# Four query-feature tasks moved from a gate pass to the down product, with later exponentials, copied-out gates and late stores

## The chip, the cores and the metric

The kernel runs on one core of one Trainium2 chip. The metric is the device time of one execution in microseconds (us). The engines are TensorE (PE), VectorE (DVE), ScalarE (ACT), GpSimd (POOL) and SyncE (SP), whose queue issues nearly all transfers. Each works through its own instructions in order and waits for others by semaphores.

## The reference

A token matrix x of 2048 rows and 1024 columns is layer-normed; the result xn goes through a linear attention with learned features, and through a gated unit; both results are combined with x.

```python
qkv = xn @ wqkv                          # 32 heads of 32
pq, pk = q @ w_phi, k @ w_phi            # per head
phi_q = concat([softmax(pq), softmax(-pq)])
phi_k = concat([softmax(pk), softmax(-pk)])
kv = phi_k^T v ;  z = sum over rows of phi_k
o = (phi_q kv) / (phi_q z + 1e-6)
s = o @ wo
g = silu((sigmoid(xn @ w_gate) * (xn @ w_up)) @ w_down)   # 3584 columns inside
out = x + s * g
```

Everything is fp32. A softmax pair over the 32 values of a head is computed as: the maximum and the minimum (the extremes), the two differences (the spread), the exponential of both, sums and their inverses.

## The kernel before

**Products.** A matrix product in fp32 is made of three matmuls (`mm3`, lines 145 to 147). Each operand is first split (`split`, lines 136 and 137): ACT casts it to the short form, DVE subtracts that from the original. A large product is cut into 2 x 2 blocks and done with seven block products in place of eight; they are named B11, B21, T1 to T4 and B22, and partial results are carried from one to the next in the eight PSUM banks.

**Stages, in order of time.** Layer norm and the weights' sums (to about 310 us, with the first projections among them), the first gate pass (about 310 to 580), projections (to 820), the second gate pass (T2, T3 and T4 of the gated unit, to 1300), the third (T1 and B22, to 1593), the down product (112 steps of `dsteps`, 2352 matmuls, to 2134), and last the attention's output with the product by `wo`, eight pairs of row tiles, whose order is written out word by word in the lists `PAIR` and `LAST`.

**Order of the work.** Around the matmuls stands a plan: `later(n, f)` puts a piece of work n ticks ahead, and `tick()` is called between groups of matmuls and runs what is due. In the down product a tick is 12 matmuls, 2.72 us; in the nests of the third pass 18 ticks are 65 us. A scheduler then sets the final order on each engine; a piece of work may be held to a place behind matmuls already written.

**Feature tasks.** Raw keys, queries and values lie in `qkv_d`. A key task (`k_steps`, second pass) loads a tile, takes extremes, spread, exponential (line 677), inverses, scales, and ends in the key products `kv_products` on PE, which read the low halves that line 729 writes. A query task handles row tile t and column half hb, 32 tasks in all. `q_steps` (early) makes extremes (lines 663 and 664), spread (673 and 674), exponential and inverses (682 and 683) during a gate pass and stores the exponentials in `e_d` and the inverses in `r_d`. `q_late` runs in the down product for all 32 tasks: a light one only loads `e_d` and `r_d`; a heavy one loads the raw queries and does the features there. Both then weigh with z (POOL, line 995), form the density (DVE, 1000 to 1006), scale (POOL, 1013) and store to `e_d`. In the kernel before, the tasks of t = 0 to 7 are early: t up to 5 in the first pass, t = 6 and 7 in the third.

**Nests of the third pass.** A gate product is itself done by seven smaller block products. In `nest`, line 1612 (`nc.scalar.copy(a, c)` in the middle of `product(T3, ...)` and `product(T4, ...)`) copies one bank to another on ACT; the matmuls of T4 wait for it. `h_added` (lines 1437 to 1439) adds on DVE and takes the sigmoid on ACT.

**The second pass.** `keep_bank` (line 1396) copies a bank out on ACT and `seed` (line 1392) copies a stored part into a bank; the next matmuls into that bank wait for either.

**The down product.** Operands are loaded, split by `down_prep` into free buffers some steps ahead, and used in the order of `dsteps`. When a product's last step has written bank p, `evacuate(i, p)` takes the bank's result out. `gate_out` forms silu as y times sigmoid(y) and stores to `g_d`.

**The end.** In `PAIR`, a word eUH loads a tile of `e_d` into buffer U (`e_load`, line 1042), trUHQ transposes it on PE (line 1052), and w0 to w3 load `wo` for B22 into the block `x0` (line 1037) in the first pair. That block held results of the down product before.

Of the kernel before, what the change touches and what calls it, by code (L numbers as in the profile page):

```python
# [11 lines left out]
F32R = mybir.dt.float32r  # L12
AF = mybir.ActivationFunctionType
# [14 lines left out]
HB = 512  # L28
# [21 lines left out]
def hedgehog_glu_kernel(  # L50
# [63 lines left out]
    LEAD = 2  # L114
    KAT, CQ = 0, 7
    BEHIND = 'DVE', 'Activation', 'SP'
# [314 lines left out]
    FLY = range(2, NJ - 1)  # L431
    WD_B, WD_C = range(10), ()
    last_raw, raw_free, spare, groups, made_sums = [], deque(), [], deque(), {}
# [242 lines left out]
    def exponentials(e):  # L676
        nc.scalar.activation(e, e, AF.Exp)  # L677
# [61 lines left out]
    def k_steps(at, hb, t):  # L739

        wide = int((hb, t) >= (0, EARLY))
        for n, f in ((0, k_load), (4, k_extremes), (5, k_spread), (7, lambda *a: exponentials(e_k)),
                     (9, k_inverses), (10, k_scale), (11, k_low), (13 + (1 + wide) * (t < TT - 1), kv_products)):
            later(max(at + n, 1), f, hb, t)
# [202 lines left out]
    def q_steps(at, t, hb):  # L947

        def load():
            p, e = hold[:] = qf_raw.next(), whole(qf_e.next())  # L950
            nc.sync.dma_start(p, qkv_d[Q, t, hb])

        def first():
            hold.append(extremes(f"q{t}{hb}", hold[0]))

        def sums():
            hold.append(inverses(hold[2], hold[1]))

        def keep():
            nc.sync.dma_start(r_d[t, hb], hold[3])  # L960
            nc.sync.dma_start(e_d[t, hb], hold[1])

        hold = []
        for n, f in ((0, load), (5, first), (6, lambda: spread(hold[2], *hold[:2])), (7, lambda: exponentials(hold[1])),
                     (8, sums), (9, keep)):
            later(at + n, f)

    def q_late(at, t, hb):
# [3 lines left out]
        def load():  # L972
            if t < CTT:
                hold["e"] = whole(eqr.next())
                nc.sync.dma_start(hold["e"], e_d[t, hb])
                hold["r"] = small.tile([P, 32], F32, name=f"r{t}{hb}", tag="r", bufs=2)
                nc.sync.dma_start(hold["r"], r_d[t, hb])
            else:
                hold["p"] = qraw.next()
                nc.sync.dma_start(hold["p"], qkv_d[Q, t, hb])  # L980
# [37 lines left out]
        heavy = ((5, first), (6, second), (9, lambda: exponentials(hold["e"])), (11, sums))  # L1018
        steps = ((0, load),) + heavy if t >= CTT else ((6, load),)
        for n, f in steps + ((11, weigh), (14, density), (15, scale), (18, keep)):  # L1020
# [440 lines left out]
    def begin_pass(p):  # L1461

        if p == 0:
# [6 lines left out]
            for n in range(12):  # L1470
                q_steps(5 + 6 * n, n // 2, n % 2)
            for n, f, *a in ((1, x_nest_sums, 0, 1), (2, x_nest_split, 0, T2, (1,)), (2, x_nest_split, 0, T3, (1,)),
# [3 lines left out]
        elif p == 1:  # L1476
            gates_r.items = halves(45, 46)
            gates_r.n = 0
            for n, f, *a in ((152, x_nest_load, 2, 0, 0), (153, x_nest_load, 2, 0, 1), (154, x_nest_load, 2, 1, 0),
                             (159, x_nest_load, 2, 1, 1), (158, x_nest_sums, 2, 0), (163, x_nest_sums, 2, 1),  # L1480
                             (164, x_nest_split, 2, T4, (0,)), (165, x_nest_split, 2, T4, (1,)), (166, x_nest_split, 2, T2), (169, x_nest_split, 2, T3)):
                later(n, f, *a)
            at = KAT
            for t in range(EARLY, 2 * TT):
                k_steps(at, *divmod(t, TT))
                at += 6
                if t % TT == TT - 1:
                    k_end(at + 7, t // TT)
                    at += 18
        else:  # L1490
            for n, j in enumerate(WD_C):
                queue2(40 + 16 * n, wd_sums, j, halves(53, 54))
            qf_raw.items, qf_e.items = [slots[50][:, 1]], [52]
            for n in range(4):
                q_steps(CQ + 18 * n, 6 + n // 2, n % 2)

# [293 lines left out]

    def gate_out(y, t, i, fused=None):

        if fused is None:
            m = sig_r.next()
            nc.scalar.activation(m, y, AF.Sigmoid)
            nc.gpsimd.tensor_mul(y, y, m)  # L1796
        else:
            nc.scalar.activation(y, fused, AF.Sigmoid)
            nc.vector.tensor_mul(y, y, fused)
        nc.sync.dma_start(g_d[t, :, i * HB:(i + 1) * HB], y)  # L1800

    def evacuate(i, p):
# [10 lines left out]
        elif i in (T2, T3):  # L1813
            nc.scalar.copy((u1 if i == T2 else u2)[p], b)
        elif i == T4:
            gate_out(yr.next(), t + 4, 0, b)
        elif i == T1:
            nc.vector.tensor_add(u2[p], u2[p], b)
            later(1 + p, gate_out, u2[p], t + 4, 1)
        else:  # L1820
            nc.vector.tensor_add(u1[p], u1[p], b)
            gate_out(u1[p], t, 1)
# [3 lines left out]
    for hb in range(2):  # L1826
        later(1 + hb, nc.sync.dma_start, zb[hb], zb_d[hb])
    for n in range(TT):
        for hb in range(2):
            q_late(2 + (2 * n + hb) * 24 // 5, n // 2 + n % 2 * CTT, hb)  # L1830
    for n, (i, j, cs) in enumerate(dsteps):
# [52 lines left out]
    res.items = halves(49, 52, 43, 38)  # L1884
    block("x0", 0, 4, F32R)

# [88 lines left out]
    def last_block():  # L1975
# [7 lines left out]
        for h in halved:  # L1983
            nc.vector.tensor_mul(y[:, h], g[:, h], ps[:, h])
            nc.vector.tensor_add(y[:, h], y[:, h], left[:, h])  # L1985
            nc.sync.dma_start(out[t * P:(t + 1) * P, cols.start + h.start:cols.start + h.stop], y[:, h])

    operand_of = dict(B11=B11, B21=B21, T2=T2, T3=T3, T4=T4, T1=T1, B22=B22)
    i_ = lambda n: operand_of[n]
# [11 lines left out]
        (r"y(\w+)", False, lambda p, i: store(p, i_(i))),  # L2001
        (r"w(\d)", False, lambda p, k: p or wo_prep(B22, int(k))),
        (r"rest", False, lambda p: last_rest()),
# [47 lines left out]
```

## Time and profile before

| | us |
|---|---|
| median of three runs | 2351.31 |
| lowest, highest | 2346.94, 2352.96 |
| profiled execution, own time | 2349.81 |
| its span in the trace | 2348.0 |
| mean granted PE clock | 0.998 |

| engine | busy us | share |
|---|---|---|
| PE | 2328.9 | 99% |
| DVE | 1691.8 | 72% |
| ACT | 1246.7 | 53% |
| POOL | 1114.6 | 47% |
| DMA queue q1 | | 78.4% of 16 engines |

A row of the timeline gives the start, the duration, the engine, the line of the kernel, the operation with the tiles written and read, and in brackets the idle time before it and what ended that. A row of a stretch gives busy time and the count of instructions of each engine, then the granted clock of PE, the share of the DMA engines and GB/s. A row of a group gives count, total, mean in nanoseconds, and idle time before.

### The profile page before, as it was taken

How to read it: one execution, taken by the hardware profiler on the slowest of the kernel's cores; microseconds unless marked ns; L12 is line 12 of the kernel's file. 1: busy time of each engine (PE TensorE's matmuls, PEld its weight loads, DVE VectorE, ACT ScalarE, POOL GpSimd, SP SyncE). 2: the span in 40 equal slices, each digit the busy share in tenths (PEclk: the TensorE clock that was granted, in tenths of full speed). 3: DMA queues.
4: the chain of work that ended last, by engine and by line, in shares of the span. 5: the costliest groups of instructions: out<-in, count | busy, mean ns of one | idle time of the engine just before them, and what ended most of it. 6: DMA issues, size and time to landing. Idle time of an engine off the chain costs nothing. (4 is left out here: it accounts for less than half of the span.)

```text
span 2348.0 us, 32662 instructions
## 1 busy us (share of the span) xinstructions
PE 2328.9 (99%) x10816; PEld 1941.1 (83%) x10816; DVE 1691.8 (72%) x2147; ACT 1246.7 (53%) x2003; POOL 1114.6 (47%) x801
## 2 busy tenths in 40 slices
PE   9999999999999999999999999999999999999999
PEld 8888888888888888888888878778888888888887
DVE  8625677776888764777864766674899889876776
ACT  7354577776555555555555555553444444355553
POOL 0323436781231054664663667654665434424556
PEclk9999999999999999999999999999999999999999
DMA  8789987988888777897896877769877667785665
GB/s 298 255 310 360 339 292 275 352 317 300 280 275 286 267 252 271 303 312 256 279 323 204 294 251 237 239 240 354 289 255 262 227 205 253 251 278 199 204 199 184
DMA packets 305017, 635.68 MB, mean 271 GB/s; under 512 B 38608, under 2 KB 38864, under 8 KB 300240
## 3 DMA queue, kind: packets, MB, share of 16 engines
q1 hardware_dynamic: 304848, 633.60, 78.4%
q8 instruction: 84, 1.38, 0.2%
q14 instruction: 85, 0.70, 0.1%
HBM read 380.50 MB, written 252.97 MB: 270 GB/s over the span
## 5 line engine op out<-in xcount | busy, mean ns | idle before, releaser
L145 PE MATMUL bank<-x,w 128*128 128x512 f32 x2248 | 875.9, 390 | 2.4 <-ACT fc L1396 1.9
L146 PE MATMUL bank<-x,w 128*128 128x512 f32 x2248 | 876.0, 390 | 0.0
L147 PE MATMUL bank<-x,w 128*128 128x512 f32 x2248 | 875.1, 390 | 0.0
L137 DVE TENSOR_TENSOR w<-fa,w 128x512 fp32r<-128x512 f32 (+2 forms) x394 | 390.2, 996 | 298.4 <-ACT w L136 288.3
L145 PEld LDWEIGHTS bank<-x,w 128*128 128x128 f32 x2248 | 422.9, 188 | 90.4 <-ACT fc L1396 2.3
L147 PEld LDWEIGHTS bank<-x,w 128*128 128x128 f32 x2248 | 422.6, 188 | 87.4
L146 PEld LDWEIGHTS bank<-x,w 128*128 128x128 f32 x2248 | 422.6, 188 | 87.2
L136 ACT CAST w<-fa 128x512 fp32r<-128x512 f32 (+2 forms) x394 | 268.8, 684 | 335.9 <-PE bank L146 221.3
L145 PE MATMUL bank<-w,x 128*128 128x512 f32 x708 | 277.4, 392 | 0.0
L147 PE MATMUL bank<-w,x 128*128 128x512 f32 x708 | 276.1, 390 | 0.0
L146 PE MATMUL bank<-w,x 128*128 128x512 f32 x708 | 276.0, 390 | 0.0
L137 DVE TENSOR_TENSOR w<-fb,w 128x512 fp32r<-128x512 f32 (+1 forms) x116 | 106.4, 918 | 78.8 <-ACT w L136 78.6
L147 PEld LDWEIGHTS bank<-w,x 128*128 128x128 f32 x708 | 132.9, 188 | 27.7 <-DVE x L1252 0.3
L146 PEld LDWEIGHTS bank<-w,x 128*128 128x128 f32 x708 | 133.0, 188 | 26.8 <-DVE w L1262 0.4
L145 PEld LDWEIGHTS bank<-w,x 128*128 128x128 f32 x708 | 133.1, 188 | 26.1
L136 ACT CAST w<-fb 128x512 fp32r<-128x512 f32 (+1 forms) x116 | 70.2, 605 | 113.7 <-PE bank L146 90.3
L137 DVE TENSOR_TENSOR x<-fb,x 128x512 fp32r<-128x512 f32 (+1 forms) x87 | 88.6, 1022 | 25.0 <-ACT x L136 24.5
L1396 ACT COPY fc<-bank 128x512 f32<-128x512 f32 x116 | 66.5, 584 | 40.6 <-PE bank L147 18.7
L137 DVE TENSOR_TENSOR p<-fc,p 128x512 fp32r<-128x512 f32 (+1 forms) x68 | 50.8, 758 | 40.2 <-ACT p L136 38.2
L1090 POOL TENSOR_TENSOR fc<-fc 128x512 f32<-128x512 f32 x32 | 48.8, 1526 | 62.3 <-DVE fb L1101 20.4
L136 ACT CAST x<-fb 128x512 fp32r<-128x512 f32 (+1 forms) x87 | 65.4, 754 | 12.7 <-DMA fb<-xr_d 5.5
L677 ACT ACTIVATE fc<-fc 128x1024 f32<-128x1024 f32 x36 | 38.2, 1061 | 48.8 <-DVE fc L674 48.6
(412 smaller groups left out, 3822.5 us busy)
## 6 DMA issues: line engine op xcount, KB each, us to landing
m_d<-fc SPq DMA_DIRECT2D x168, 256.0 KB, 4.2
fa<-h_d SPq DMA_DIRECT2D x152, 256.0 KB, 4.3
fa<-wf_d SPq DMA_DIRECT2D x32, 1024.0 KB, 6.8
x<-m_d SPq DMA_DIRECT2D x128, 256.0 KB, 4.9
fa<-w_gu SPq DMA_DIRECT2D x102, 256.0 KB, 5.1
h_d<-fc SPq DMA_DIRECT2D x102, 256.0 KB, 5.0
fc<-e_d SPq DMA_DIRECT2D x48, 512.0 KB, 5.7
fc<-qkv_d SPq DMA_DIRECT2D x88, 256.0 KB, 5.1
```

Source lines behind the costliest of these rows:

```text
L136: nc.scalar.copy(o[0], src)
L137: i = nc.vector.tensor_sub(o[1], src, o[0].bitcast(F32))
L145: nc.tensor.matmul(o, a[0], b[0], start=first, stop=False, **kw)
L146: nc.tensor.matmul(o, a[0], b[1], start=False, stop=False, **kw)
L147: last_mm[:] = [nc.tensor.matmul(o, a[1], b[0], start=False, stop=last, **kw).ins]
L677: nc.scalar.activation(e, e, AF.Exp)
L1090: nc.gpsimd.tensor_sub(o, a, b)
L1396: nc.scalar.copy(o, banks[b])
```

## The change

Line numbers of the changed kernel are a few lower behind line 1480 (1612 becomes 1606, 1800 becomes 1792, 1900 becomes 1897).

1. Query tasks of t = 6 and 7, both halves, are no longer done in the third pass. `QA = 6` takes the place of `CTT` (8) in `q_late`, so that there are 12 light and 20 heavy tasks in the down product, where there were 16 and 16. They no longer alternate: of eight tasks in a row, the third, the sixth and the eighth are light.
2. In key tasks and in early query tasks the exponential comes three ticks after the spread for keys and two for queries, one more than before. The early query tasks as a whole start a tick sooner, so that load, extremes and spread come a tick sooner and the rest at the same tick as before.
3. T4's results in the down product are copied out of their banks, odd ones by ACT and even ones by DVE. Then `gate_out` is put on the plan (sigmoid on ACT, product on POOL). Before, ACT took the sigmoid from the bank and DVE multiplied with the bank.
4. The last four stores to `g_d` that the down product makes for B22 (tiles 8 to 11) wait in a list until w0 in the first pair, ahead of the loads of `wo` into `x0`.

```diff
-    KAT, CQ = 0, 7
+    QA = 6
...
     def k_steps(at, hb, t):
-        for n, f in ((0, k_load), (4, k_extremes), (5, k_spread), (7, lambda *a: exponentials(e_k)),
+        for n, f in ((0, k_load), (4, k_extremes), (5, k_spread), (8, lambda *a: exponentials(e_k)),
                      (9, k_inverses), (10, k_scale), (11, k_low), (13 + (1 + wide) * (t < TT - 1), kv_products)):
...
-        for n, f in ((0, load), (5, first), (6, lambda: spread(hold[2], *hold[:2])), (7, lambda: exponentials(hold[1])),
-                     (8, sums), (9, keep)):
+        for n, f in ((0, load), (5, first), (6, lambda: spread(hold[2], *hold[:2])), (8, lambda: exponentials(hold[1])),
+                     (9, sums), (10, keep)):
             later(at + n, f)
...
     def q_late(at, t, hb):
-            if t < CTT:
+            if t < QA:
...
-        steps = ((0, load),) + heavy if t >= CTT else ((6, load),)
+        steps = ((0, load),) + heavy if t >= QA else ((6, load),)
...
-                q_steps(5 + 6 * n, n // 2, n % 2)
+                q_steps(4 + 6 * n, n // 2, n % 2)
...
-        else:
-            for n, j in enumerate(WD_C):
-                queue2(40 + 16 * n, wd_sums, j, halves(53, 54))
-            qf_raw.items, qf_e.items = [slots[50][:, 1]], [52]
-            for n in range(4):
-                q_steps(CQ + 18 * n, 6 + n // 2, n % 2)
...
+    last_stores = []
+
+    def gate_out(y, t, i):
+
+        m = sig_r.next()
+        nc.scalar.activation(m, y, AF.Sigmoid)
+        nc.gpsimd.tensor_mul(y, y, m)
+        store = lambda: nc.sync.dma_start(g_d[t, :, i * HB:(i + 1) * HB], y)
+        if len(dready) == ND and i == 1 and t >= CTT and t < CTT + 4:
+            last_stores.append(store)
         else:
+            store()
...
         elif i == T4:
-            gate_out(yr.next(), t + 4, 0, b)
+            y = yr.next()
+            (nc.scalar.copy if p % 2 else nc.vector.tensor_copy)(y, b)
+            later(1 + (p + 1) // 2, gate_out, y, t + 4, 0)
...
-    for n in range(TT):
-        for hb in range(2):
-            q_late(2 + (2 * n + hb) * 24 // 5, n // 2 + n % 2 * CTT, hb)
+    light, heavy = [deque((t, hb) for t in ts for hb in range(2)) for ts in (range(QA), range(QA, TT))]
+    for n in range(2 * TT):
+        q_late(2 + n * 24 // 5, *(light if (n + 1) * QA // TT > n * QA // TT else heavy).popleft())
...
-    block("x0", 0, 4, F32R)
...
+    def last_weights(k):
+        if k == 0:
+            for store in last_stores:
+                store()
+            block("x0", 0, 4, F32R)
+        wo_prep(B22, k)
...
-        (r"w(\d)", False, lambda p, k: p or wo_prep(B22, int(k))),
+        (r"w(\d)", False, lambda p, k: p or last_weights(int(k))),
```

What this does to the order of instructions is shown at four places. In the rows, a name's first number is that of the buffer.

ACT in the third pass, in the nest about 1404 us, before:

```order
L1571 COPY bank0_101<-bank4_105 128x512
L1575 ACTIVATE x5_3_9819<-x5_3_9819 128x512
L677 ACT_TABLE_LOAD
L677 ACTIVATE fc_0_100<-fc_0_100 128x1024
L1612 COPY bank4_105<-bank6_107 128x512
L1439 ACT_TABLE_LOAD
L1439 ACTIVATE fb_0_99<-fb_0_99 128x512
L136 CAST w_0_94<-fa_0_97 128x512
```

The same nest after:

```order
L1565 COPY bank0_101<-bank4_105 128x512
L1569 ACTIVATE x5_3_9819<-x5_3_9819 128x512
L136 CAST w_0_94<-fa_0_97 128x256
L1439 ACTIVATE fb_0_99<-fb_0_99 128x512
L1606 COPY bank4_105<-bank6_107 128x512
L136 CAST w_0_94<-fa_0_97 128x512
```

The query task's exponential and two table loads are gone; the gate's sigmoid now stands ahead of the bank copy, and a cast has come ahead of both.

ACT in the second pass, about 1097 us, before:

```order
L1396 COPY fc_0_100<-bank0_101 128x512
L677 ACT_TABLE_LOAD
L677 ACTIVATE fc_0_100<-fc_0_100 128x1024
L136 CAST w_0_94<-fb_0_99 128x512
L1396 COPY fc_0_100<-bank1_102 128x512
L1396 COPY fc_0_100<-bank2_103 128x512
```

After:

```order
L1396 COPY fc_0_100<-bank0_101 128x512
L136 CAST w_0_94<-fb_0_99 128x512
L677 ACT_TABLE_LOAD
L677 ACTIVATE fc_0_100<-fc_0_100 128x1024
L1396 COPY fc_0_100<-bank1_102 128x512
L1396 COPY fc_0_100<-bank2_103 128x512
```

The cast has moved ahead of the table load and the exponential; the copies of banks 1 and 2 still stand behind it.

SP at the start of the final pairs, before (`x2` is two alike in a row):

```order
L1800 DMA g_d<-x_5_12069 128x512 x2
L1900 DMA fc_100<-g_d 128x512
L1800 DMA g_d<-x_5_12069 128x512 x2
L1042 DMA fc_100<-e_d 128x1024 x2
L1037 DMA x_6_16229<-wo_d 128x1024 x4
```

After:

```order
L1037 DMA x_2_5939<-wo_d 128x1024
L1897 DMA fc_100<-g_d 128x512
L1042 DMA fc_100<-e_d 128x1024 x2
L1792 DMA g_d<-x_5_12025 128x512 x4
L1037 DMA x_6_16313<-wo_d 128x1024 x4
```

The four stores have moved behind the two loads from `e_d`.

DVE in the down product, about 1766 us, before (stq101 and sa101 belong to the heavy task of tile 10, half 1; the line 137 rows are splits):

```order
L663 TENSOR_REDUCE stq101_13311<-fb_0_99 128x16
L664 TENSOR_REDUCE stq101_13311<-fb_0_99 128x16
L1001 TENSOR_TENSOR sa21_13303<-sa21_13303,r21_13119 128x32
L137 TENSOR_TENSOR x4_2_5939<-fa_0_97,x4_2_5939 128x512
L1003 TENSOR_REDUCE sa21_13303<-sa21_13303 128x16
L137 TENSOR_TENSOR w_0_94<-fa_0_97,w_0_94 128x512
L673 TENSOR_TENSOR x6_6_12071<-fb_0_99,stq101_13311 128x16x32
L674 TENSOR_TENSOR x6_6_12071<-stq101_13311,fb_0_99 128x16x32
L682 TENSOR_REDUCE stq100_13206<-x6_6_12071 128x32
L1004 TENSOR_SCALAR sa21_13303<-sa21_13303 128x16
L137 TENSOR_TENSOR x4_2_5939<-fa_0_97,x4_2_5939 128x512
L137 TENSOR_TENSOR w_0_94<-fa_0_97,w_0_94 128x512
```

After, the same task:

```order
L1006 TENSOR_TENSOR sa100_13571<-stq100_13396,sa100_13571 128x32
L137 TENSOR_TENSOR w_0_94<-fa_0_97,w_0_94 128x512
L663 TENSOR_REDUCE stq101_13601<-fb_0_99 128x16
L664 TENSOR_REDUCE stq101_13601<-fb_0_99 128x16
L137 TENSOR_TENSOR x4_2_5939<-fa_0_97,x4_2_5939 128x512
L673 TENSOR_TENSOR x6_6_12027<-fb_0_99,stq101_13601 128x16x32
L674 TENSOR_TENSOR x6_6_12027<-stq101_13601,fb_0_99 128x16x32
L137 TENSOR_TENSOR w_0_94<-fa_0_97,w_0_94 128x512 x2
L137 TENSOR_TENSOR x4_2_5939<-fa_0_97,x4_2_5939 128x512
L137 TENSOR_TENSOR w_0_94<-fa_0_97,w_0_94 128x512
L137 TENSOR_TENSOR w_0_94<-fb0_0_98,w_0_94 128x512
```

The spread of this task was followed at once by the sums of the task before it (stq100); now those have been done, with the density of that task too (sa100), and splits follow. Across 1748 to 1786 us the heavy rows have moved apart in this way.

More of the change, by code (lines that the diff above doesn't have):

```diff
@@ L431, in hedgehog_glu_kernel @@
     FLY = range(2, NJ - 1)
-    WD_B, WD_C = range(10), ()
+    WD_B = range(10)
     last_raw, raw_free, spare, groups, made_sums = [], deque(), [], deque(), {}
@@ L1482, in begin_pass @@
                 later(n, f, *a)
-            at = KAT
+            at = 0
             for t in range(EARLY, 2 * TT):
@@ L1789, in hedgehog_glu_kernel @@
     u1, u2 = halves(0, 1, 2, 3), halves(4, 5, 6, 7)
[L1791 to L1796, printed above, removed]
-        else:
-            nc.scalar.activation(y, fused, AF.Sigmoid)
-            nc.vector.tensor_mul(y, y, fused)
-        nc.sync.dma_start(g_d[t, :, i * HB:(i + 1) * HB], y)
+    last_stores = []
[6 more added lines that the diff above has]
+            last_stores.append(store)
+        else:
+            store()
     def evacuate(i, p):
```

## The prediction

> **What bounds the kernel now.** I read the page's first line, then what TensorE (PE) waited for, then the stretches around those waits, and last what the engine named in each wait was doing.
>
> ```profile
> PE 2328.9 (99%) x10816; PEld 1941.1 (83%) x10816; DVE 1691.8 (72%) x2147; ACT 1246.7 (53%) x2003; POOL 1114.6 (47%) x801
> ```
>
> PE is the bound from end to end: of a span of 2348.0 us it is idle for 19.1. Nothing in this change takes a matmul away, so a gain can come only out of those 19 us and out of the slow clock that follows some of them. The waits by cause (total, number, longest):
>
> ```profile
> PE bank L145 <- ACT bank L1612: 7.0, 3, 2.4
> PE bank L1052 <- DMA fc<-e_d: 2.8, 2, 2.0
> PE bank L145 <- ACT fc L1396: 1.9, 1, 1.9
> ...
> PE bank L145 <- ACT bank L1392: 0.5, 1, 0.5
> ```
>
> The first row is the third pass, the second the final pairs, the other two the second pass. Stretches of 24 us, three around the L1612 waits, an undisturbed one for comparison, and one around the L1396 wait; the last columns are granted PE clock, DMA share and GB/s:
>
> ```profile
> 1088.00:1112.00 24.00, 22.14 (x94) 17.80 (x93) 16.33 (x17) 10.59 (x17) 15.14 (x11) 0.93 0.79 261
> ...
> 1388.00:1412.00 24.00, 21.66 (x89) 17.43 (x88) 15.85 (x20) 13.65 (x22) 15.80 (x14) 0.93 0.61 199
> 1412.00:1436.00 24.00, 24.00 (x108) 19.87 (x107) 16.46 (x21) 13.01 (x24) 17.17 (x16) 1.00 0.67 231
> 1460.00:1484.00 24.00, 21.79 (x89) 17.56 (x88) 17.67 (x22) 13.95 (x22) 16.53 (x15) 0.93 0.72 240
> 1532.00:1556.00 24.00, 21.58 (x95) 17.54 (x95) 19.21 (x23) 13.73 (x23) 13.43 (x9) 1.00 0.94 322
> ```
>
> The undisturbed stretch holds 108 matmuls, 0.222 us each. Two of the disturbed ones hold 89, the third 95. So a stall costs more than its wait where the clock falls after it (0.93 over 24 us is 1.7 us of clock).
>
> **The third pass, term one.** ScalarE (ACT) around the L1612 copies:
>
> ```profile
> 1339.58 1.06 ACT L677 ACTIVATE fc<-fc 128x1024 f32<-128x1024 f32 x1
> ...
> 1399.64 1.28 ACT L677 ACT_TABLE_LOAD   x1
> 1403.42 1.06 ACT L677 ACTIVATE fc<-fc 128x1024 f32<-128x1024 f32 x1 [2.49 <-DVE fc L674]
> 1404.38 0.58 ACT L1612 COPY bank<-bank 128x512 f32<-128x512 f32 x1
> ...
> 1424.76 0.63 ACT L1439 ACTIVATE fc<-fc 128x512 f32<-128x512 f32 x1 [1.72 <-DVE fc L1437]
> 1425.30 0.58 ACT L1612 COPY bank<-bank 128x512 f32<-128x512 f32 x1
> ...
> 1468.73 1.06 ACT L677 ACTIVATE fc<-fc 128x1024 f32<-128x1024 f32 x1 [2.48 <-DVE fc L674]
> ...
> 1534.18 1.06 ACT L677 ACTIVATE fc<-fc 128x1024 f32<-128x1024 f32 x1 [3.59 <-DVE fc L674]
> ```
>
> ACT works in order. The exponential of a query task waits 2.5, 2.5 and 3.6 us for VectorE's (DVE's) spread, and the bank copy behind it, which PE needs, waits along. The four exponentials are these tasks; the first (1339.58) came without a wait, the other three make the three stalls. The copies between them (1425.30) stand in the order that the changed kernel has everywhere here, the gate's sigmoid ahead of the copy, and no PE wait is listed for them. So I expect all three stalls to go. Worth: the waits alone are 7.0; with 1.7 us of slow clock after two of them 10.4; by missing matmuls 19 + 19 + 13 = 51 at 0.222 it is 11.3. I take 10.9 and keep 7.0 and 11.3 as ends. With the tasks go 4 loads, 8 stores, 4 exponentials and their table loads; PE waits for no other DMA there, so these are worth 0.
>
> The Trainium skill, "TensorE: Matmul & The Clock Gate", Part 1 (What's actually happening), says that the clock halves after at least one idle window of about 3.4 us. By that, gaps of at most 2.4 us cost no clock, term one is its lower end, 7.0, and the sum about 10. The granted 0.93 in two stretches does not agree with it, and I go by the stretches.
>
> **The second pass, term two.** The exponential moves one tick later, and here is what that meets:
>
> ```profile
> 1097.07 1.28 ACT L677 ACT_TABLE_LOAD   x1 [3.73 <-DVE fc L674]
> 1098.37 1.06 ACT L677 ACTIVATE fc<-fc 128x1024 f32<-128x1024 f32 x1
> 1099.33 0.60 ACT L136 CAST w<-fb 128x512 fp32r<-128x512 f32 x1
> 1099.84 1.06 ACT L1396 COPY fc<-bank 128x512 f32<-128x512 f32 x2
> ```
>
> The order shows that only the CAST gets ahead of the exponential, into the 3.73 us in which ACT was waiting anyway; the copy of bank 1, for which PE waits, still stands behind it. The copy starts at 1099.33 in place of 1099.84, 0.5 us sooner, and a wait of 1.4 stays. Whether the clock still falls after it (1.7 us) I can't tell; half of it is 0.85. The 0.5 us wait on L1392 should go, since that copy now precedes a CAST that waits for GpSimd (POOL). Ends: 0.5 (the CAST alone) and 0.5 + 0.5 + 1.7 = 2.7. I take 1.6. Exponentials elsewhere in this pass get behind one CAST that can wait for PE; the inverse that follows is two ticks on in the old schedule and one in the new, so I price that at 0, with up to 2 us against me if a key product comes late. In the first pass the query tasks' exponentials keep their tick and only loads, extremes and spread come a tick sooner; no wait of PE is listed there, price 0.
>
> **The end, term three.** In the first pair of the last lists:
>
> ```profile
> 2138.27 2.54 POOL L1796 TENSOR_TENSOR x<-x,p 128x512 f32<-128x512 f32 x2
> ```
>
> ```profile
> 2139.59 1.57 SPq L1800 DMA_DIRECT2D g_d<-x  x2
> 2141.25 0.89 SPq L1042 DMA_DIRECT2D fc<-e_d  x2
> ```
>
> ```profile
> 2139.38 0.60 PE L1052 MATMUL bank<-ident,fc 128*128 128x128 f32 x4
> ...
> 2140.50 0.60 PE L1052 MATMUL bank<-ident,fc 128*128 128x128 f32 x4
> ```
>
> The last store waits for POOL's product, done at 2140.81, and the two loads from e_d stand behind it in SP's queue. In the changed order they stand ahead of all four stores, so they are held only by the transposes that read their buffers (done at 2139.98 and 2141.10). The first, whose late landing is the 2.0 us wait, leaves 1.25 us sooner and without 512 KB of stores just ahead of it. I take 1.6 of that wait, with 0 and 2.8 (both e_d waits) as ends. The weight loads into x0 wait in turn for the stores to land, some 3 us later than now; they are used at the far end of the first pair's list, and I price that at 0.
>
> **The down product, term four.** What comes in is four heavy tasks in place of light ones. The durations, over 1600 to 2065 us:
>
> ```profile
> L682 DVE TENSOR_REDUCE stq<-x 128x32 f32<-128x1024 f32 x16 | 19.3, 1209 | 0.0
> ...
> L673 DVE TENSOR_TENSOR x<-fc,stq 128x512 f32<-128x512 f32 x8 | 8.9, 1109 | 0.0
> ...
> L674 DVE TENSOR_TENSOR x<-stq,fc 128x512 f32<-128x512 f32 x8 | 8.2, 1030 | 0.0
> ...
> L683 DVE RECIPROCAL stq<-stq 128x32 f32<-128x32 f32 x16 | 5.5, 341 | 0.0
> ...
> L663 DVE TENSOR_REDUCE stq<-fc 128x16 f32<-128x512 f32 x8 | 5.4, 675 | 0.0
> ...
> L1810 DVE COPY fc<-bank 128x512 f32<-128x512 f32 x6 | 3.9, 677 | 0.0
> L1799 DVE TENSOR_TENSOR fc<-fc,bank 128x512 f32<-128x512 f32 x6 | 3.8, 673 | 0.0
> ```
>
> ```profile
> 1753.00:1805.00 52.00, 52.00 (x231) 43.04 (x231) 51.62 (x70) 25.82 (x41) 35.02 (x24) 1.00 0.78 257
> ...
> 1600.00:2065.00 465.00, 465.00 (x2053) 385.02 (x2053) 398.93 (x569) 205.61 (x338) 224.47 (x160) 1.00 0.77 261
> ```
>
> A heavy task takes DVE 0.675 twice (the two extremes) + 1.109 + 1.030 + 1.209 + 0.341 = 5.0 us; four take 20. T4 copied out takes four DVE copies (2.7) in place of eight products (5.4). Net +17.3 on DVE, 398.9 to 416 of 465. ACT gets 4 exponentials of 1.06 and 4 copies more, about 7 on 206; POOL gets 8 products, the tasks' loads are half as large, SP issues four fewer. All of this lies beside PE, which is busy for all of the 465 us; what hides it is the lead of the prepared operands over PE. That lead is thin at one place, in the first of the two stretches:
>
> ```profile
> 1770.82 0.68 DVE L137 TENSOR_TENSOR x<-fa,x 128x512 fp32r<-128x512 f32 x1
> ```
>
> ```profile
> 1772.55 0.39 PE L145 MATMUL bank<-x,w 128*128 128x512 f32 x1
> ```
>
> The operand ready at 1771.50 is read at 1772.55: 1.05 us to spare, with DVE busy for 51.62 of 52. In the changed order the heavy rows stand more evenly at just that place: with the mean durations, the DVE work queued for the two fullest steps there falls from 11.9 and 10.1 us to 9.0 and 8.2, though some 15 us more has been done by the end of the stretch. I take 0. Ends: 0, since PE loses nothing there now, and 10, worked out under the first rival. T1's first matmuls need T4's banks: one copy (0.68) frees a bank no later than sigmoid and product did, price 0.
>
> **The sum.** 10.9 + 1.6 + 1.6 - 0 = 14.1 us less. The profiled execution took 2349.81 us, 1.5 below the median of the runs (2351.31); against it that is 2335.7, against the median 2337.2. I say 2336.5, about 0.6% faster. A change of 0.3% (7 us) is about what a measurement of this kernel can tell from none.
>
> **Rivals.** First, DVE becomes the bound in the down product. For it: 17.3 us of new work, and one stretch with 0.4 us idle. What sets the price is how long DVE takes beside POOL:
>
> ```profile
> 1752.01 0.68 DVE L673 TENSOR_TENSOR x<-fc,stq 128x512 f32<-128x512 f32 x1
> 1752.61 1.78 DVE L674 TENSOR_TENSOR x<-stq,fc 128x512 f32<-128x512 f32 x1
> ```
>
> Twin instructions take 0.68 and 1.78. If each of the eight added ones took the long time, that is 8 x 0.72 (1.78 less the mean 1.06), 6 us more; a few per cent on the other products would use up the lead. Then PE loses what DVE overruns, some 6 us, and slow clock after two gaps, 3.4: about 10 back, 2346.5. Against it: nowhere in those 465 us did PE wait, even with 1.05 us of lead.
>
> The Trainium skill, "SBUF — State Buffer", section "SBUF: two separate sides", says that a DVE instruction with two SBUF inputs and a GpSimd one lock each other out for a whole instruction. By the eight new POOL products could hold DVE up by their full length, at 1.27 us each (half of the 2.54 above) 10 in all; they come late in the product, after the thin place.
>
> Second, slower than before: in the down product ACT's exponentials, now 20, hold back the casts and bank copies behind them as they did in the third pass, the moved tasks taking their stall along. A stall costs about 2 us of wait and 1.7 of clock, 3.7. From four such stalls the gain is gone, from six the kernel is slower by over 0.3%; with eight, 30 - 14 = 16 slower, 2366. For it: the exponentials there already wait for DVE. Against it: no bank is waited for at that place, and the operands lead.
>
> Third, the later exponentials and the late stores do nothing, because the exponential still stands ahead of the bank copy and the load's landing, not its issue, is what is late. Then only 10.9 is won, 2339.7 on the scale of my 2336.5. With it I count that the lost clock isn't the stalls' own, so that term one is worth 7.0 and the time 2340.4; two stretches at 0.93 around two stalls leave that about 0.03.
>
> **Chances.** Forecast 0.54, its own range 2331 to 2341; third rival 0.18; first 0.16; second 0.12. Faster by over 0.3% are the forecast and the third, 0.72; the first is within 0.3%, 0.16; the second is slower, 0.12. The range 2330 to 2349 takes in the ends of terms one to three and the 10 of the down product, and leaves out the second rival and a little.
>
> **What would show it.** Term one: no wait on L1606 (the copy's new line) in the third pass, and 108 matmuls with clock 1.00 in each 24 us stretch of it. Term two: a wait on the copy of bank 1 (L1396) of 1.4 us, none on L1392. Term three: the e_d loads ahead of the stores, their wait 0.4 or less in the first pair. Term four: no PE wait between 1590 and 2120 us; DVE at about 416 us over 465 of them. It would be wrong if waits on casts or DVE products (L136, L137) appear in the down product with clock below 1.00, or if key products in the second pass wait for L729.

## The result, and the profile after

| | before | changed |
|---|---|---|
| median, us | 2351.49 (6 runs) | 2332.62 (6 runs) |
| lowest, highest | 2346.94, 2352.96 | 2331.74, 2334.36 |
| profiled execution, its span | 2349.81, 2348.0 | 2333.20, 2331.4 |

The ratio is 0.9923, 95% interval 0.9910 to 0.9936: 0.77% or 18.9 us faster, where 14.1 us were forecast. The two profiled executions lie 16.6 us apart.

What PE waited for in the changed kernel, all of it (total, number, longest):

```profile
PE bank L1326 <- POOL ident masks.py:199: 1.5, 1, 1.5
PE bank L380 <- DMA fb<-wqkT: 0.7, 1, 0.7
PE bank L1052 <- DMA fc<-e_d: 0.6, 1, 0.6
PE bank L145 <- ACT fc L1396: 0.5, 1, 0.5
PE bank L145 <- ACT bank L1392: 0.5, 1, 0.5
PE bank L145 <- DVE x L1819: 0.3, 1, 0.3
```

The row on line 1612, now 1606, is gone; the second pass and the end keep 0.5 + 0.5 and 0.6. The three stretches of 24 us of the third pass where the stalls were, and the one of the second pass:

```profile
1383.00:1407.00 24.00, 24.00 (x108) 19.88 (x107) 14.78 (x21) 12.39 (x23) 17.09 (x16) 1.00 0.64 208
1449.00:1473.00 24.00, 24.00 (x108) 19.88 (x107) 11.52 (x17) 11.65 (x22) 17.24 (x15) 1.00 0.68 225
1510.00:1534.00 24.00, 24.00 (x108) 19.88 (x107) 14.12 (x17) 11.60 (x21) 22.21 (x18) 1.00 0.75 239
1088.00:1112.00 24.00, 23.46 (x111) 19.16 (x110) 20.01 (x19) 12.06 (x20) 14.12 (x10) 1.00 0.81 267
```

108 matmuls and clock 1.00 in the third pass, as in an undisturbed stretch. Comparing the start of the same PE instruction in both traces gives where the 16.6 us went: opening with the first pass and the projections 0.5, second pass 2.3, third pass 11.2, down product 0.0, end 2.6. The opening varies from one execution to the next: its part up to 310 us takes up to 2.0 us more in other traces of kernels whose opening is the changed kernel's. The down product, changed kernel:

```profile
1753.00:1805.00 52.00, 52.00 (x231) 43.07 (x230) 51.06 (x78) 21.96 (x37) 26.75 (x21) 1.00 0.79 265
...
1588.00:2053.00 465.00, 465.00 (x2054) 385.18 (x2053) 415.20 (x591) 209.97 (x346) 236.01 (x167) 1.00 0.76 259
```

PE is busy for all of the 465 us; DVE for 415.2 of them.

### The profile page after: what moved, and what is told of

It reads as the page before. It is cut to its first block, busy times and chain, and to the rows that moved or that the text cites. A ratio compares the mean times of both kernels' runs of the same rounds, so it can differ in the third digit from the quotient of the medians.

```text
span 2331.4 us, 32661 instructions
## 1 busy us (share of the span) xinstructions
PE 2322.5 (100%) x10816; PEld 1938.1 (83%) x10816; DVE 1715.9 (74%) x2143; ACT 1236.0 (53%) x1997; POOL 1130.0 (48%) x809
## 4 chain that ended last, share of the span: by engine, by line
PE 94%; DMA 2%; DVE 1%; POOL 1%; ACT 1%; issue 1%; SPq 0%; POOLq 0%; ACTq 0%; DVEq 0%
PE bank L145 29%; PE bank L147 29%; PE bank L146 29%; PE bank L1076 1%; PE bank L1052 1%; PE bank L735 1%; PE bank L380 1%; PE bank L1326 0%; DMA wf_d<-p 0%; DMA fa<-w_gu 0%; DMA fb<-wqkT 0%; DMA fa<-wf_d 0%; PE bank L248 0%; DMA fc<-e_d 0%; POOL p L1299 0%
## 5 line engine op out<-in xcount | busy, mean ns | idle before, releaser
L137 DVE TENSOR_TENSOR w<-fa,w 128x512 fp32r<-128x512 f32 (+2 forms) x394 | 396.1, 1011 | 276.3 <-ACT w L136 269.6
L137 DVE TENSOR_TENSOR p<-fc,p 128x512 fp32r<-128x512 f32 (+1 forms) x68 | 55.7, 829 | 39.3 <-ACT p L136 37.2
L136 ACT CAST x<-fb 128x512 fp32r<-128x512 f32 (+1 forms) x87 | 65.3, 753 | 13.3 <-DMA fb<-xr_d 5.2
L677 ACT ACTIVATE fc<-fc 128x1024 f32<-128x1024 f32 x44 | 46.6, 1060 | 36.2 <-DVE fc L674 36.0
```

The source lines that it names most:

```text
L136: nc.scalar.copy(o[0], src)
L137: i = nc.vector.tensor_sub(o[1], src, o[0].bitcast(F32))
```

## The experiments

All times are medians of five runs or more, against 2350.5 to 2351.5 for the kernel before beside them. The changed kernel itself was run again beside the last three:

> The changed kernel once more, on the same chip as the three beside it, to tell their small differences from those between chips and calls: 2332.6, within 1.5 us.

It took 2332.31 us (2331.56 to 2334.89).

**The moved tasks alone.** The first part of the diff on the kernel before:

```diff
-                q_steps(CQ + 18 * n, 6 + n // 2, n % 2)
...
-            q_late(2 + (2 * n + hb) * 24 // 5, n // 2 + n % 2 * CTT, hb)
+        q_late(2 + n * 24 // 5, *(light if (n + 1) * QA // TT > n * QA // TT else heavy).popleft())
```

> The kernel before with the first part alone: the four query tasks of t = 6 and 7 go from the third pass to the down product (12 light, 20 heavy, in the new order); exponentials, T4 and stores as before. Theory: the three stalls of the third pass go with the tasks, about 11 us, and the down product hides their DVE work: 2351.5 - 11 = 2340 to 2341, no wait on the bank copy in the third pass, none in the down product, the wait of 1.9 us at 1100 us and the two e_d waits as before. Rival (the down product gives part back): 2343 or more, with waits on splits there.

2340.12 us, 10.7 less than the 2350.78 beside it, ratio 0.9949 (0.9937 to 0.9962). The waits:

```profile
PE bank L1052 <- DMA fc<-e_d: 2.4, 1, 2.4
PE bank L145 <- ACT fc L1396: 1.8, 1, 1.8
...
PE bank L145 <- ACT bank L1392: 1.3, 2, 1.1
```

No bank copy of the third pass is waited for, none in the down product; the other two places stall much as before. Term one is this part, and it carries more than half of the gain.

**The later exponentials alone.** The tasks stay in the third pass:

```diff
-(7, lambda *a: exponentials(e_k)),
+(8, lambda *a: exponentials(e_k)),
...
-(7, lambda: exponentials(hold[1])),
-                     (8, sums), (9, keep)):
+(8, lambda: exponentials(hold[1])),
+                     (9, sums), (10, keep)):
...
-                q_steps(5 + 6 * n, n // 2, n % 2)
+                q_steps(4 + 6 * n, n // 2, n % 2)
```

> The kernel before with the second part alone: exponentials one tick later in key tasks and early query tasks; the four query tasks stay in the third pass. In the order the exponential there now stands some six rows behind the bank copy for which PE waited, with the spread by then long done. Theory A (what cost the time was only the place of the waiting exponential ahead of the copy): the three stalls go here too, 11 us, and with the 2 us of the second pass the time is 2338 to 2339; moving the tasks was then not needed for them. Theory B (the tasks' own work on ACT and DVE delays the copies): waits of about 2 us on the bank copy stay, 2349. A middle way: the exponential with its two table loads (1.06 + 2 x 1.28 us) now stands ahead of another copy (line 1571) and makes a new, smaller wait there.

2350.26 us, ratio 1.000 (0.9991 to 1.0009). Theory A falls. The part is not without effect, though: between the same matmuls of the two traces, the second pass is 3.3 us shorter than before and the third 4.6 us longer. PE's longest wait, and ACT before it:

```profile
PE bank L145 <- ACT bank L1592: 9.9, 4, 3.4
```

```profile
1345.21 1.28 ACT L677 ACT_TABLE_LOAD   x1
1346.50 1.06 ACT L677 ACTIVATE fc<-fc 128x1024 f32<-128x1024 f32 x1
1347.58 1.28 ACT L1575 ACT_TABLE_LOAD   x1
1348.88 0.63 ACT L1575 ACTIVATE x<-x 128x512 f32<-128x512 f32 x1
1349.41 0.58 ACT L1571 COPY bank<-bank 128x512 f32<-128x512 f32 x1
1349.93 0.55 ACT L1592 COPY bank<-bank 128x512 f32<-128x512 f32 x1
```

The exponential no longer waits for anything, and still four stalls are there, one for each task, on another copy. Its 1.06 us with a table load ahead of it and another for the gate's sigmoid behind it hold ACT for 3.7 us, and in these four nests a copy that PE waits for stands close behind. So it was neither the spread alone nor the place alone: in this order each of the four exponentials costs a stall, where before the one that came without a wait (1339.58) cost none. That is the middle way of the expectation, though not a smaller wait.

**The changed kernel with the old exponentials.** First both kinds, then the key tasks' alone (the first of the two lines turned back):

```diff
-(8, lambda *a: exponentials(e_k)),
+(7, lambda *a: exponentials(e_k)),
```

> The changed kernel without its second part: exponentials at their old tick in key tasks and early query tasks. Theory: the second pass gets its stall back, a wait of about 1.9 us on the copy of bank 1 with 1.7 us of slow clock, and waits of 0.5 to 1.1 us on L1392, in place of 0.5 + 0.5 us: 2332.6 + 2 to 4 = 2334.5 to 2336.5. Rival (the second pass's stalls come from GpSimd's late sums and not from the exponential): 2332.6, within 1 us.

> The changed kernel with the key tasks' exponentials alone at their old tick; the early query tasks of the first pass stay as changed. Theory (the exponential ahead of the copies on L1392 and L1396 is what exp_early lost): both waits of some 2 us at 1100 and 1130 us are there again and the time is 2336 to 2338.5, like exp_early. Rival (part of exp_early's loss lies in the first pass, from the query tasks): 2334 to 2335.5.

2338.31 us (2335.72 to 2338.60) and 2337.84 us (2336.81 to 2339.16), ratios 0.9942 and 0.9946 to before, where the changed kernel has 0.9923 and 0.9925. The two don't differ, so by the medians the effect is the key tasks', 5.5 us (2337.84 - 2332.31) where term two forecast 1.6. The rows of the first, then of the second:

```profile
PE bank L145 <- ACT bank L1392: 2.0, 1, 2.0
PE bank L145 <- ACT fc L1396: 1.8, 1, 1.8
```

```profile
PE bank L1052 <- DMA fc<-e_d: 2.4, 5, 0.6
PE bank L145 <- ACT fc L1396: 2.4, 2, 1.8
```

The wait on the copy at 1099 us is there in its old size in both profiles. In the second the clock was at half for 3.4 us after it, in the first it was not. The second stall, at 1130 us, came back in the first only. The time of the first lies above the 2336.5 that I had expected at most.

Not all of the 5.5 us lies where the exponentials are. Between the same matmuls, the second pass takes 2.3 to 2.6 us more than in the profiled changed kernel in the four traces with the old exponentials (before, the tasks alone, and these two). In the eight other traces with the exponentials of the change (the later exponentials alone, the repeat and the runs below, except the next one) it takes 1.0 to 2.5 us less. The median difference is 3.8 us. The rest of the 5.5 is mostly in small waits at the end of the second kernel, 2.4 in place of 0.6 or 1.2 in the two traces of the changed kernel. Nothing shows that they hang on the exponentials: the end varies by up to 3.9 us between traces with the same stores.

**A tick later still.** Exponential, inverses, scale and low part one tick later, and the earliest key products too. The sum over key products is then taken before those of the last tile are in, so that this kernel's attention leaves them out; the instructions are the same in number.

```diff
-(8, lambda *a: exponentials(e_k)),
-                     (9, k_inverses), (10, k_scale), (11, k_low), (13 + (1 + wide) * (t < TT - 1), kv_products)):
+(9, lambda *a: exponentials(e_k)),
+                     (10, k_inverses), (11, k_scale), (12, k_low), (14 + wide * (t < TT - 1), kv_products)):
```

> The changed kernel with the key tasks' exponential, inverses, scale and low part one tick later still (the key products one tick later where they were earliest). In the order the exponential now stands ahead of the sigmoid of line 1429 and behind the copy of bank 2, with one more pair of table loads. Theory (a wait comes from whatever stands behind an exponential with its table loads): the 0.5 us on L1396 and L1392 go, but 2 x 1.28 us more of table loads per task can make new waits on the copy of bank 3 or on the product after the sigmoid: 2331.5 to 2336. If nothing stands close behind it, 2331.5.

2351.99 us. It fell outside of what I expected, and not by ACT's copies:

```profile
PE bank L735 <- DVE p L729: 13.3, 6, 5.5
```

The key products now wait for the low halves, 13.3 us in six waits. One tick later was free, the second is not: the changed kernel sits at the edge of what the key products' lead allows.

**T4 as before, in the changed kernel.**

```diff
-            (nc.scalar.copy if p % 2 else nc.vector.tensor_copy)(y, b)
-            later(1 + (p + 1) // 2, gate_out, y, t + 4, 0)
+            nc.scalar.activation(y, b, AF.Sigmoid)
+            nc.vector.tensor_mul(y, y, b)
+            nc.sync.dma_start(g_d[t + 4, :, :HB], y)
```

> The changed kernel without its third part: T4's results are gated from their banks by ACT and DVE, as before. Theory (all of it lies beside PE, and a copy frees a bank no later than sigmoid and product): 2332.6, within 1 us, with no PE wait in the down product, DVE 2.7 us more there and POOL some 12 us less. Rival (the copies free the banks sooner, which now matters since DVE has more to do): waits on DVE products between T4 and T1, 1 to 4 us more, 2334 to 2337.

2332.97 us (2332.57 to 2335.02), no difference from 2332.31 or 2332.62. PE waits for nothing there in either. But the load on DVE is not what I had summed:

```profile
1588.00:2053.00 465.00, 465.00 (x2053) 385.04 (x2052) 407.19 (x596) 209.10 (x343) 222.28 (x159) 1.00 0.77 259
```

Copying T4 out takes 2.7 us of instructions off DVE and yet DVE is busy for 8.0 us more (415.2 against 407.2), with POOL busy for 13.7 more. What makes up for it is longer instructions beside POOL: in the down product of the changed kernel, a split that no POOL instruction overlaps takes 0.68 us (126 of them, none over 0.69), one that is overlapped 1.1 on average and up to 1.83 (133 of them). How much it adds up to varies: over the same matmuls, five more traces with T4 copied out have DVE busy for 410.6 to 413.4 us, and the kernel with the tasks alone, T4 as before, for 408.0. So the products on POOL stretch DVE by some 5 to 11 us. The Trainium skill ("SBUF — State Buffer", section "SBUF: two separate sides") says that a DVE instruction with two SBUF inputs and a GpSimd one that reads SBUF lock each other out; this trace agrees in the direction, and the 10 us that the prediction worked out lie within that range.

It cost no time, since the operands' lead over PE does not fall to nothing. The smallest lead in T1's steps, after:

```profile
1979.38 1.52 DVE L137 TENSOR_TENSOR x<-fb,x 128x512 fp32r<-128x512 f32 x1
```

```profile
1981.82 0.39 PE L146 MATMUL bank<-x,w 128*128 128x512 f32 x1
```

By the places in the block that the two write and read, this matmul is the first to read the low half that this split makes: 0.9 us to spare. With T4 as before the same operand has 6.1.

**Stores not held back, in the changed kernel.**

```diff
-        if len(dready) == ND and i == 1 and t >= CTT and t < CTT + 4:
+        if False:
...
+    block("x0", 0, 4, F32R)
...
-            block("x0", 0, 4, F32R)
```

> The changed kernel without its fourth part: the last four stores of g_d at once, as before. Theory (the loads from e_d stand behind a store that waits for GpSimd): the first wait grows from 0.6 us to about 2.0 and the second, of 0.8 us, comes back: 2332.6 + 2.2 = 2334.5 to 2335.5. Rival (the load's landing and not its issue is late): 2332.6 and the same waits as in the changed kernel.

2334.89 us (2332.87 to 2336.44), 2.3 to 2.6 more than the changed kernel, which is not clear of the noise: the intervals of the ratios overlap (0.9914 to 0.9939 against 0.9910 to 0.9936), and so do the runs. In the trace the first wait is 1.8:

```profile
PE bank L1052 <- DMA fc<-e_d: 1.8, 1, 1.8
```

against 0.6 in the changed kernel, 1.2 more, which is close to the 1.25 us by which the load was to issue sooner. The second wait of before (0.8 at 2256 us) did not come back, so these stores alone do not make it. Over all traces, the end (the last 220 us) takes a median of 1.5 us more in the four with early stores than in the ten with late ones, but the two groups overlap.

**More heavy tasks, until something gives.** `QA` is 2 and then 0, so that 28 and 32 tasks are heavy, and the early ones are fewer to match (28 is the one labelled four less: eight more than in the changed kernel, with four early tasks left):

```diff
-    QA = 6
+    QA = 2
...
-            for n in range(12):
+            for n in range(2 * QA):
```

> The changed kernel with only 4 early query tasks (tiles 0 and 1): 28 heavy tasks in the down product, 8 more, DVE 415 + 40 = 455 of 465 us. Theory: fits on the mean, so at most local overruns once the lead is used up: 2332 to 2340. If DVE's durations grow beside POOL as in the first rival of the prediction, the overrun comes already here: 2340 to 2350.

> The changed kernel with no early query task at all: all 32 are heavy in the down product, 12 more, none in the first pass. DVE's work in the down product grows from 415 us over 465 by 12 x 5.0 = 60 to 475, more than there is time. Theory (the lead of the prepared operands hides DVE's work as long as it fits): PE now waits on splits, 10 us of overrun plus slow clock after the gaps, minus at most 10 us of lead: 2335 to 2360, with waits on L137 from the thin place on. Rival (the exponentials hold ACT and with it casts and bank copies): PE waits on casts, several gaps of 2 to 3 us with slow clock, 2350 to 2380. Should nothing wait, DVE has more room than its busy share says, 2332.

2339.49 and 2343.97 us. At last PE waits in the down product; the rows of the kernel with 32 heavy tasks:

```profile
PE bank L145 <- ACT bank L1807: 4.7, 1, 4.7
PE bank L146 <- DVE x L137: 1.9, 2, 1.5
...
PE bank L145 <- ACT x L1813: 1.3, 1, 1.3
PE bank L147 <- DVE w L137: 0.5, 1, 0.5
```

With 28, the first row alone is there (4.0 us). ACT and DVE in that wait, with 28:

```profile
1735.06 1.19 ACT L1807 COPY bank<-x 128x512 f32<-128x512 f32 x2 [2.80 <-DVE fc L1806]
```

```profile
1733.22 1.21 DVE L1000 TENSOR_REDUCE sa<-fc 128x32 f32<-128x1024 f32 x1
1734.35 1.28 DVE L1806 COPY fc<-bank 128x512 f32<-128x512 f32 x2
```

No wait on a split is listed there: the operands still lead, but B21's finished banks stand at the end of the same, late queue. DVE copies them out, ACT writes the next start value (line 1807), and PE waits for both. To test that, the banks are copied out by ACT in the kernel with 28:

```diff
-            nc.vector.tensor_copy(y, b)
+            nc.scalar.copy(y, b)
             nc.scalar.copy(b, u1[p])
```

> The kernel with 28 heavy tasks (heavy_4_less) and B21's eight banks copied out by ACT in place of DVE. Theory (with 28 heavy tasks PE waits only because DVE's late queue also holds the bank copies at the one change of products, line 1806, and not for splits): the wait of 4.0 us on L1807 at 1732 us goes or falls below 1.5, no wait on L137 comes, 2332.5 to 2335. Rival (DVE's lag would have stopped PE anyway, at the next split): 2337 to 2340 with waits on L137.

The wait falls from 4.0 to 1.1, and no wait on a split comes in its place:

```profile
PE bank L145 <- ACT bank L1807: 1.1, 1, 1.1
PE bank L145 <- ACT bank L1392: 1.0, 1, 1.0
PE bank L145 <- ACT bank L1586: 0.8, 1, 0.8
```

The cause of that wait is thereby shown. The time, 2337.30 us, between 2332.75 and 2338.28, is above what I expected and would not have told it. In the profiled run, which took 2337.30, the down product is only 1.4 us longer than in the changed kernel, where it was 7.0 with the banks copied by DVE; but the part up to 310 us, which has the copy on L1586, is 4.1 us longer. Whether the ACT copies have to do with that isn't known.

**Heavy tasks in one run.** Twelve light tasks first, then the twenty heavy:

```diff
-        q_late(2 + n * 24 // 5, *(light if (n + 1) * QA // TT > n * QA // TT else heavy).popleft())
+        q_late(2 + n * 24 // 5, *tasks[n])
```

> The changed kernel with its 12 light tasks first and then the 20 heavy ones in one run, in place of the even mix. In the heavy stretch (some 260 us) DVE has about 8.5 us of other work per 13.06 us and 5.0 for a heavy task, 13.5: 0.4 us too much each time, 9 us in all. Theory (the even mix is what keeps the lead): PE loses between 0 and 10 us late in the down product, 2333 to 2343. Rival (order does not matter): 2332.6.

2332.75 us (2332.62 to 2335.03): no difference. Five stretches in a row are like these two, and PE lost 0.2 us in all:

```profile
1805.00:1857.00 52.00, 52.00 (x231) 43.06 (x230) 51.21 (x79) 22.82 (x38) 19.98 (x16) 1.00 0.61 195
...
1909.00:1961.00 52.00, 52.00 (x231) 43.03 (x231) 51.28 (x79) 23.57 (x38) 21.63 (x17) 1.00 0.60 195
```

So the mix isn't needed for the time: DVE at 51.3 of 52 us keeps up with PE. It does keep a lead, though. Here the lead is used up late in the product, and this matmul starts 0.06 us after the split of its operand is done:

```profile
2013.70 0.50 PE L147 MATMUL bank<-x,w 128*128 128x512 f32 x1 [0.20 <-DVE w L137]
```

POOL's share in the two stretches is lower than elsewhere, which may be part of how DVE keeps up; no run tests it.

## Why the prediction was right, point by point

The forecast was 14.1 us, the likeliest way came, and the measured 18.9 lies inside the range. By the steps:

- **Term one** said 10.9 between 7.0 and 11.3. The part alone gave 10.7, the traces 11.2. The slow clock after the stalls is their own, as the stretches had said, and the lower end of 7.0 fell with it. So did the reading by the Trainium skill ("TensorE: Matmul & The Clock Gate", Part 1, What's actually happening), by which such gaps cost no clock. Why these tasks stall was told too narrowly. I named the wait for the spread; the run with later exponentials shows that without that wait the exponential and its two table loads make a stall of the same size.
- **Term two** is the one that was mis-sized: 1.6 forecast, at most 2.7. The two profiled executions give 2.3 in the second pass, all traces together a median of 3.8, and the medians of the runs 5.5, of which the rest isn't shown to be the exponentials'. The step that failed is "a wait of 1.4 stays". In the profiled changed kernel 0.5 stayed on that copy, in the eight other traces with these exponentials no wait on it is listed at all, and the slow clock never came there. I had moved ACT's rows and held PE's arrival fixed. Measured from the cast that waits for GpSimd some 7 us ahead (1091.71 before, 1090.18 after), PE came to that copy 0.8 us later in the changed trace, and the copy 0.5 us sooner. The forecast that L1392's wait goes was wrong: 0.5 is still there in the profiled run, and 0.2 to 1.0 in most others.
- **Term three** said 1.6 between 0 and 2.8. The medians give 2.3 to 2.6, not clear of the noise, the wait itself 1.2, the end as a whole 1.5. Price 0 for the later weight loads held: nothing waits for line 1037.
- **Term four** said 0 and was 0, but the margin was thinner than it said. The thin place was read nearly right: the split that ends at 1771.50 makes the low half of an operand, which line 145 does not read yet, but line 146 does:

```profile
1772.78 0.39 PE L146 MATMUL bank<-x,w 128*128 128x512 f32 x1
```

So 1.28 us were to spare and not 1.05, the smallest lead in the down product before. As forecast, the new order relieves that place, to 2.9 us. But the lead got thin at two others, 0.9 us at 1732 and at 1981 us, which the prediction had not looked at; that it held there is partly luck. DVE's total of 416 (415.2 measured) was right by luck too, by two wrong sizes. The four tasks alone raised it by about 9 (407.8 in the kernel with that part alone, 1591 to 2056, against 398.9), not 20, and T4's copies by some 3 to 9, not -2.7.

The rows show what takes back the 11 in the first of the two: the spreads of the four tasks (lines 673 and 674) were priced at 8.6 and added 3.6, since all spread rows became shorter (0.92 us on average, 1.04 before); the splits took 3.8 less; and rows that follow one another without a pause overlap in the trace, which takes another 2.7 off the busy time.

- **The first rival**, DVE as the bound with about 10 us given back, did not come with 20 heavy tasks. With 28 and 32 it came at 7 and 11 us, mostly by a door that I had not named, the bank copies behind DVE's late queue; with 32, waits on splits (1.9 and 0.5) come beside it. **The second**, exponentials that hold ACT, is what happens in the third pass. In the down product it does not come with 20 heavy tasks, but with all 32 heavy it is there once, in the wait of 1.3 us on line 1813. ACT ahead of that copy, with 32 heavy:

```profile
1972.24 1.28 ACT L677 ACT_TABLE_LOAD   x1
1973.54 1.06 ACT L677 ACTIVATE x<-x 128x1024 f32<-128x1024 f32 x1
1974.62 1.28 ACT L1790 ACT_TABLE_LOAD   x1
1975.91 0.63 ACT L1790 ACTIVATE fb<-fc 128x512 f32<-128x512 f32 x1
1976.45 0.57 ACT L1813 COPY x<-bank 128x512 f32<-128x512 f32 x1
```

**The third** fell in its first half: the later exponentials bring 3.8 us or more. For the late stores it is open, with 1.2 to 2.6 us by the different measures and none clear of the noise.

10.7 + 5.5 + 2.4 + 0 for T4 makes 18.6 of the 18.9. That this comes out so close is partly luck, since two of the three were got by taking a part out of the changed kernel and hold some 2 us of scatter. The parts don't simply add up either: the later exponentials alone brought nothing, because what they won in the second pass they lost in the third, where the tasks still were.

## What to carry to other kernels

Where the bounding engine is busy for 99%, the whole gain is in its few waits, and each is priced by the matmuls missing from a stretch, not by the wait alone. A function switch on ACT costs the engine its table loads on either side (1.28 us each here), so the place to put one is where nothing that PE waits for stands behind it; shifting it by a tick can move the stall to the next copy without shrinking it. To judge how much more an engine can take beside PE, look at its share less than at what else stands in its queue: operands forgive a backlog as long as they have any lead left, a bank copy between two products doesn't. And to judge a part of a change by a difference of 2 to 5 us, compare the stretch where it acts in several traces, since the opening and the end vary by as much.

## What the runs showed of the hardware

The clock fell to half for 3.41 us (in two cases 6.83) after some gaps and not after others, and the length of the gap alone does not tell which. The starts of the slow stretches in the trace of before, 1101.55, 1405.34 and 1470.19, are 89 and 19 times 3.413 us apart, so they lie on one grid. Windows cut on that grid, before (columns as above; the third number before the end is the clock):

```profile
1401.93:1405.34 3.41, 1.07 (x5) 0.58 (x4) 2.40 (x4) 1.90 (x3) 0.31 (x1) 1.00 0.79 257
1405.34:1408.75 3.41, 3.41 (x9) 2.64 (x8) 2.66 (x5) 2.48 (x4) 0.00 (x0) 0.50 0.94 294
1531.63:1535.04 3.41, 1.73 (x8) 1.11 (x6) 3.12 (x3) 0.86 (x1) 1.89 (x2) 1.00 1.05 405
1535.04:1538.45 3.41, 2.67 (x12) 2.21 (x13) 2.66 (x5) 3.15 (x6) 0.53 (x1) 1.00 0.93 314
1538.45:1541.86 3.41, 3.41 (x17) 2.83 (x16) 3.41 (x3) 2.08 (x4) 2.46 (x2) 1.00 0.87 315
```

A gap of 2.34 us inside one window leaves PE busy for 1.07 of 3.41, and the next window runs at half clock with 9 matmuls. A longer one of 2.42 us is cut in two by the grid (1.69 and 0.73), leaves 1.73 and 2.67, and nothing follows. Over the traces here the clock fell after windows with 1.85 us or more of a gap in them (1.85, 1.86, 2.08, 2.17, 2.34, 2.43 and more), not with 1.74 or less, and once not with 1.92; the ends of matmuls are modelled, so the border is not sharper than that. So a gap well under 3.4 us can cost 1.7 us of clock, and whether it does hangs on where it falls; this is luck that differs from trace to trace (the wait of 1.8 to 1.9 us on line 1396 was followed by a slow stretch in two of the four traces that have it), and is part of why terms of 2 us were hard to size.
